# Grouped-query attention: two-pair-deep PV, K transposes after PV, and q transposed on the tensor engine instead of by DMA

## The chip, the cores and the metric

One NeuronCore of one Trainium2 chip runs the whole program. The metric is device microseconds of one execution, lower is better.

In names of engines PE is TensorE, PEld the loading of its weights, DVE is VectorE, ACT is ScalarE, POOL is GpSimd and SP is the queue that issues the DMAs. S, PT, PV and the other short names are the steps of the kernel, explained below.

## The reference

```python
B, Hq, Hkv, Sq, Sk, D = 16, 32, 8, 16, 2048, 128     # q, k, v = normal * 0.05, bf16
k = jnp.repeat(k, Hq // Hkv, axis=1)
v = jnp.repeat(v, Hq // Hkv, axis=1)
scores = jnp.einsum("bhqd,bhkd->bhqk", q, k) * D ** -0.5
p = softmax(scores, axis=-1)
return jnp.einsum("bhqk,bhkd->bhqd", p, v)
```

Four query heads share one K/V head, so each K/V head serves 4 x 16 = 64 rows of q. There are 128 K/V heads. The kernel takes two at a time: 64 pairs, and each pair fills 128 rows. K and V are 134.2 MB, q and the output 2.1 MB each, so at least 138.4 MB must move.

## The kernel before

For every pair p, these steps run. `KT`: PE transposes the two K heads (32 matmuls with an identity) into staging banks of PSUM, and DVE evicts them (four `kte`). `S`: 8 matmuls give the scores. `max`: DVE scales the scores into SBUF and finds the minimum of the negated scores. `exp`: ACT. `PT`: PE transposes P (16 matmuls), ACT evicts them (two `pte`). `PV`: 32 matmuls. `norm`: O is multiplied by the reciprocal of the row sum. The order is fixed on each engine:

```python
    for kk in range(0, last_std + 1):          # PE
        if kk < NP:
            pe_prog.append(("S", kk))
        if kk >= 1:
            pe_prog.append(("PT", kk - 1))
        pe_kt(kk)                               # both K transposes of pair kk + 2
        if kk >= 1:
            pe_prog.append(("PV", kk - 1))
    ...
    for kk in range(0, last_std + 1):          # ACT
        if kk >= 1:
            act_prog += pte(kk - 1)
        if kk < NP:
            act_prog.append(("exp", kk))
        if kk >= 1:
            act_prog.append(("norm", kk - 1))
```

All transposes share three staging banks (`NSTAGE = 3`), so a transpose of 8 tiles waits until the bank filled three steps earlier has been evicted:

```python
            def wait_bank_free(ld):
                u = ld["u"]
                if u >= NSTAGE:
                    prev = loads[u - NSTAGE]
                    pe.wait_ge(sem_ev[prev["eng"]], prev["eidx"])
```

q arrives already transposed, 512 rows (four pairs) at a time, by a DMA transpose. K has 8 buffers (4 pairs), V 12 (6 pairs); at step t the SP queue issues K(t), then V(t - DV), then the store of t - DSTORE:

```python
            def issue_q(c):
                sp.dma_start_transpose(QT[:, qch * c:qch * (c + 1)], qf[qch * c:qch * (c + 1), :]).then_inc(sem_q[c], 16)
```

## Time and profile before

| | before |
|---|---|
| time, median of 13 runs | 380.33 us (379.37 to 380.83) |
| PE / DVE / ACT busy | 86% / 81% / 72% |
| start of the first S, of the last S | 8.65 us, 367.6 us |
| gap from one S to the next, steady | 5.60 us |
| last V packet landed | 365.3 us of a 379.0 us span |

Busy times of the page of the kernel before, then its DMA rows (busy tenths and GB/s in 40 equal slices of the span), then its chain of waits by engine (shares of the span).

```profile
PE 325.3 (86%) x5632; PEld 257.3 (68%) x5632; DVE 307.9 (81%) x453; ACT 272.5 (72%) x316; POOL 1.0 (0%) x6
...
DMA  7999999999999999999999999999999999999950
GB/s 253 343 405 345 407 409 350 410 340 408 363 397 406 345 408 347 404 412 346 412 342 407 366 389 405 354 406 346 412 406 345 411 339 414 406 409 410 408 201 12
...
PE 56%; ACT 30%; DMA 6%; issue 3%; SPq 2%; DVE 1%
```

The DMA digits are 9 throughout, yet the bytes moved swing between about 410 and 345 GB/s. Where the rate is low, a q transpose is in flight: from the fourth slice to the last dip, each low slice comes about 12 us after SP issued a transpose, which is the median time from its issue to its landing, and the slices in which SP issues one run at 404 to 412. So the stream slows with the transfer, not with the issuing. The digits alone would hide that. The Trainium skill ("Perfetto Trace Analysis", "Identifying the Most-Contended Engine") warns that occupancy is misleading for DMA because there are 16 DMA engines; this trace agrees that it misleads, with the same digit 9 at 410 and at 345 GB/s.

The chain of waits of the kernel before between 150 and 185 us: start, length, and what that piece was. One loop of it is shown.

```profile
161.86 1.95 ACT PT L394 x2
163.81 0.14 issue
163.94 1.05 PE ST_ps L300 x16
165.00 1.01 PE O_ps L343 x32
166.01 0.86 PE S_ps L312 x8
166.87 0.57 PE ST_ps L328 x8
167.44 0.02 issue
```

These seven pieces add up to 5.60 us. PE waits for ACT to evict the P transposes, because K transposes need the same three banks (L300 are K transposes, L328 P transposes, L343 PV, L312 S). Then the waits view of the kernel before (who waited for whom: us in total, times, longest):

```profile
ACT PT L394 <- PE ST_ps L328: 66.1, 61, 3.1
DVE Sneg L374 <- PE S_ps L312: 55.7, 62, 2.0
PE ST_ps L300 <- ACT PT L394: 34.3, 113, 0.4
```

No engine is full; each waits for another once per loop.

### The profile page before, as it was taken

What the parts mean: (1) busy time and instruction counts of PE and PEld (TensorE: products, weight loads), DVE (VectorE), ACT (ScalarE), POOL (GpSimd) and SP (SyncE); (2) the same over time, 40 slices, a digit from 0 to 9 for tenths busy, and PEclk for the clock granted to TensorE, in tenths of its full rate; (3) what the DMA queues carried; (4) which work ended last, traced back from release to release, by engine and by line L of the source; (5) the groups of instructions that cost most, each with busy time, mean ns of one, the idle gap of its engine ahead of it and who ended that gap; (6) DMA issues with size and microseconds to landing.
All of it is one profiled execution on the core that took longest, in us unless ns stands there. A gap on an engine that the chain in (4) does not pass through costs nothing.

```text
span 379.0 us, 12914 instructions
## 1 busy us (share of the span) xinstructions
PE 325.3 (86%) x5632; PEld 257.3 (68%) x5632; DVE 307.9 (81%) x453; ACT 272.5 (72%) x316; POOL 1.0 (0%) x6
## 2 busy tenths in 40 slices
PE   4779889889889988888889889889888988988884
PEld 3567667677676776676767677677776766776664
DVE  2958888888898898787988888898898897898675
ACT  1357877877787787676877877787787786787882
POOL 1000000000000000000000000000000000000000
PEclk9989999999999999999999999999999999999999
DMA  7999999999999999999999999999999999999950
GB/s 253 343 405 345 407 409 350 410 340 408 363 397 406 345 408 347 404 412 346 412 342 407 366 389 405 354 406 346 412 406 345 411 339 414 406 409 410 408 201 12
DMA packets 54839, 139.25 MB, mean 367 GB/s; under 512 B 22016, under 2 KB 22016, under 8 KB 54784
## 3 DMA queue, kind: packets, MB, share of 16 engines
q1 hardware_dynamic: 54784, 138.43, 100.4%
q8 instruction: 45, 0.74, 0.8%
q14 instruction: 10, 0.08, 0.1%
HBM read 134.22 MB, written 2.10 MB: 360 GB/s over the span
## 4 chain that ended last, share of the span: by engine, by line
PE 56%; ACT 30%; DMA 6%; issue 3%; SPq 2%; DVE 1%
ACT PT L394 30%; PE O_ps L343 17%; PE ST_ps L300 16%; PE S_ps L312 14%; PE ST_ps L328 9%; DMA Kn<-in_k_dram 6%; SPq L234 1%; SPq L243 1%; DVE PT L364 1%; ACT KT L394 1%; DVE Sneg L374 0%; SPq L251 0%; DVE O L385 0%
## 5 line engine op out<-in xcount | busy, mean ns | idle before, releaser
L374 DVE TENSOR_SCALAR_CACHE_REDUCE Sneg<-S_ps 128x2048 f32<-128x2048 f32 x64 | 146.6, 2291 | 55.7 <-PE S_ps L312 55.7
L300 PE MATMUL ST_ps<-ident,Kn 128*128 128x128 bf16 x2048 | 147.7, 222 | 44.0 <-ACT PT L394 34.3
L394 ACT ACTIVATE PT<-ST_ps 128x1024 bf16<-128x1024 bf16 x124 | 120.2, 1021 | 66.1 <-PE ST_ps L328 66.1
L364 DVE COPY KT<-ST_ps 128x1024 bf16<-128x1024 bf16 x254 | 157.9, 681 | 7.7 <-PE ST_ps L300 7.7
L300 PEld LDWEIGHTS ST_ps<-ident,Kn 128*128 128x128 bf16 x2048 | 119.8, 98 | 65.2 <-issue 32.7
L398 ACT ACTIVATE P<-Sneg,nbias 128x2048 bf16<-128x2048 f32 x64 | 128.2, 2003 | 11.0 <-DVE Sneg L374 11.0
L328 PEld LDWEIGHTS ST_ps<-ident,P 128*128 128x128 bf16 x1024 | 57.3, 98 | 26.5 <-issue 25.2
L343 PE MATMUL O_ps<-Vb,PT 128*64 128x128 bf16 x2048 | 70.7, 222 | 5.2 <-ACT PT L394 1.9
L328 PE MATMUL ST_ps<-ident,P 128*128 128x128 bf16 x1024 | 68.5, 220 | 0.5 <-ACT KT L394 0.4
L343 PEld LDWEIGHTS O_ps<-Vb,PT 128*64 128x64 bf16 x2048 | 60.0, 111 | 12.5 <-DVE PT L364 2.6
L312 PE MATMUL S_ps<-KT,QT 128*64 128x512 bf16 x512 | 66.2, 379 | 1.8 <-DVE KT L364 0.9
L409 ACT ACTIVATE O<-O_ps,rrec 128x128 bf16<-128x128 f32 x61 | 22.4, 367 | 21.6 <-PE O_ps L343 21.6
L312 PEld LDWEIGHTS S_ps<-KT,QT 128*64 128x64 bf16 x512 | 25.9, 110 | 15.1 <-issue 2.3
L398 ACT ACTIVATION_READ_ACCUMULATOR P<-Sneg,nbias 128x1 f32 x64 | 12.8, 200 | 0.0
L368 DVE RECIPROCAL rrec<-rowsum 128x1 f32<-128x1 f32 x64 | 9.7, 152 | 3.2 <-ACT P L398 3.2
L374 DVE DVE_READ_ACCUMULATOR Sneg<-S_ps 128x1 f32 x64 | 5.3, 83 | 0.0
L385 DVE TENSOR_SCALAR O<-O_ps,rrec 128x128 bf16<-128x128 f32 x3 | 1.0, 348 | 2.5 <-PE O_ps L343 2.5
L394 ACT ACTIVATE KT<-ST_ps 128x1024 bf16<-128x1024 bf16 x2 | 1.9, 1020 | 1.3 <-PE ST_ps L300 1.3
L364 DVE COPY PT<-ST_ps 128x1024 bf16<-128x1024 bf16 x4 | 2.6, 684 | 0.1
L398 ACT ACT_TABLE_LOAD x1 | 1.3, 1283 | 0.7 <-PEq L424 0.7
L229 POOL TENSOR_SCALAR ident<-iota_t 128x128 bf16<-128x128 int32 x1 | 0.5, 535 | 0.1
L227 POOL IOTA iota_t<- 128x128 int32 x1 | 0.2, 234 | 0.4 <-POOLq L424 0.4
(4 smaller groups left out, 0.4 us busy)
## 6 DMA issues: line engine op xcount, KB each, us to landing
Kn<-in_k_dram SPq DMA_DIRECT2D x128, 512.0 KB, 13.0
Vb<-in_v_dram SPq DMA_DIRECT2D x128, 512.0 KB, 12.8
out_dram<-O SPq DMA_DIRECT2D x64, 32.0 KB, 12.5
QT<-in_q_dram SPq DMA_TRANSPOSE x16, 12.2
```

The costliest lines, as they stand in the source:

```text
L234: sp.dma_start_transpose(QT[:, qch * c:qch * (c + 1)], qf[qch * c:qch * (c + 1), :]).then_inc(sem_q[c], 16)
L243: sp.dma_start(Kn[s][:, :, :], k[b, h].rearrange("(a j) d -> a j d", j=J)).then_inc(sem_k[s], 16)
L300: ins = pe.transpose(stage_ap(ld["bank"], t), Kn[s][:, j, :], ident[:, :])
L312: ins = pe.matmul(S_ps[64 * gg:64 * (gg + 1), 512 * c:512 * (c + 1)], QT[:, 128 * p + 64 * gg:128 * p + 64 * (gg + 1)], kt[:, gg, 4 * c:4 ...
L328: ins = pe.transpose(stage_ap(ld["bank"], t), P[p % 2][:, 128 * j:128 * (j + 1)], ident[:, :])
L343: ins = pe.matmul(O_ps[64 * gg:64 * (gg + 1), 0:128], pt[:, j, 64 * gg:64 * (gg + 1)], Vb[g % NBV][:, j, :], start=(j == 0), stop=(j == J ...
L364: dve.tensor_copy(evac_dst(ld), stage_bank_ap(ld["bank"])).then_inc(sem_ev["dve"], 1)
L368: dve.reciprocal(rrec[:, p:p + 1], rowsum[:, p:p + 1]).then_inc(sem_rec, 1)
L374: dve.tensor_scalar(Sneg[kk % 2][:, :], S_ps[:, :], -scale, None, op0=ALU.mult, op1=ALU.min, accum_out=nbias[:, kk:kk + 1],).then_inc(sem_ ...
L394: act.activation(evac_dst(ld), stage_bank_ap(ld["bank"]), ACT.Copy).then_inc(sem_ev["act"], 1)
L398: act.activation(P[kk % 2][:, :], Sneg[kk % 2][:, :], ACT.Exp, bias=nbias[:, kk:kk + 1], scale=-1.0, accum_out=rowsum[:, kk:kk + 1],).then ...
L409: act.activation(Osb[s_][:, :], O_ps[:, 0:128], ACT.Copy, scale=rrec[:, p:p + 1]).then_inc(sem_nm["act"], 1)
```

## The change

It has two parts. The new loop comes from `hand_schedule`: PV moves one more pair behind (a third PT buffer), norm goes from ACT to DVE, and in odd cycles one of the four K evictions goes to ACT. Secondly q is loaded by a plain DMA and transposed on PE. V is issued 3 pairs behind K, not 2. A list scheduler (`build_schedule`) is also added, but never called. The core of the diff, cuts marked:

```diff
+NPT = 3
-DV = 2
+DV = 3
...
+def hand_schedule(NP, qp, pe_transposes_q):
+    """One pattern for every pair k: S(k) PT(k-1) KT(k+1,1) PV(k-2) KT(k+2,0)."""
...
+    for k in range(NP + 2):
+        if k < NP:
+            pe.append(("S", k))
+            dve.append(("max", k))
...
+        if 1 <= k <= NP:
+            pe.append(("PT", k - 1))
+            act.append(("pte", k - 1, 0))
+            (act if k < NP else dve).append(("pte", k - 1, 1))
+        if k >= 2:
+            pe.append(("PV", k - 2))
+        if k >= 1:
+            kt(k + 1, 1), kte(dve, k + 1, 1)
+        if k >= 2:
+            dve.append(("norm", k - 2))
+        kt(k + 2, 0)
+        kte(dve, k + 2, 0, (0,))
+        if k % 2 == 0:
+            kte(dve, k + 2, 0, (1,))
+        if k < NP:
+            dve.append(("recip", k))
+            act.append(("exp", k))
+        if k % 2 == 1:
+            kte(act, k + 2, 0, (1,))
+        if k % qp == qp - 3:
+            qt(k // qp + 1)
...
-                sp.dma_start_transpose(QT[:, qch * c:qch * (c + 1)], qf[qch * c:qch * (c + 1), :]).then_inc(sem_q[c], 16)
+                sp.dma_start(Qn[:, 4 * c:4 * (c + 1), :], qf[qch * c:qch * (c + 1), :].rearrange("(a j) d -> a j d", j=4)).then_inc(sem_q[c], 16)
...
+                elif op[0] == "QT":
...
+                    for j in range(4):
+                        ins = pe.transpose(stage_ap(ld["bank"], j), Qn[:, 4 * c + j, :], ident[:, :])
```

More of the change, by code (lines that the diff above doesn't have):

```diff
@@ L20 @@
 QLEAD = 6
+_DUR = {
+    "KT_load": 0.46, "PT_load": 0.46, "S": 0.75, "PV": 1.02,
+    ("dve", "kte"): 0.63, ("dve", "pte"): 0.63, ("dve", "max"): 2.30, ("dve", "recip"): 0.17, ("dve", "norm"): 0.36,
+    ("act", "kte"): 1.07, ("act", "pte"): 1.07, ("act", "exp"): 2.08, ("act", "norm"): 0.46,
+    "K": 0.65, "V": 0.65, "ST": 0.65, "Q": 3.3,
+}
+_LAT = 0.12
+_LAT_SAME = 0.04
+_DMA_LAT = 2.0
+_BW = 0.371
+_BW_SLOW = 0.364
+_RING_MB = 5.2
+_SIZE = {"K": 0.5, "V": 0.5, "Q": 0.25 * 1.45, "ST": 0.03125 * 1.45}
@@ new lines, with sp_program @@
+_T0 = 7.0
+def sp_program(NP, qch_pairs, dv=DV, dstore=DSTORE, qlead=QLEAD):
+    sp = []
+    n_qch = (NP + qch_pairs - 1) // qch_pairs
+    q_step = {c: max(0, c * qch_pairs - qlead) for c in range(n_qch)}
+    for t in range(NP + max(dv, dstore) + 1):
+        if t < NP:
+            sp += [("K", 2 * t), ("K", 2 * t + 1)]
+        for c in range(n_qch):
+            if q_step[c] == t:
+                sp.append(("Q", c))
+        if 0 <= t - dv < NP:
+            sp += [("V", 2 * (t - dv)), ("V", 2 * (t - dv) + 1)]
+        if 0 <= t - dstore < NP:
+            sp.append(("ST", t - dstore))
+    return sp
@@ new lines, with build_schedule, t, eng_options @@
+SCHED_OPTS = dict(kte_engs=("dve", "act"), pte_engs=("dve", "act"), norm_engs=("dve", "act"), eft=True)
+def build_schedule(NP, qch_pairs, nbk=NBK, nbv=NBV, nbo=NBO, nkt=NKT, npt=NPT, nstage=NSTAGE, opts=None):
+    INF = float("inf")
+    DUR = _DUR
+    opts = dict(SCHED_OPTS, **(opts or {}))
+    sp = sp_program(NP, qch_pairs)
+    done = {}
+    def t(key):
+        return done.get(key, INF)
+    pe_left = []
+    for p in range(NP):
+        pe_left += [("KT", p, 0), ("KT", p, 1), ("S", p), ("PT", p), ("PV", p)]
+    x_left = []
+    for p in range(NP):
+        x_left += [("kte", p, gg, h) for gg in range(2) for h in range(2)]
+        x_left += [("pte", p, h) for h in range(2)]
+        x_left += [("max", p), ("recip", p), ("exp", p), ("norm", p)]
+    sp_left = list(sp)
+    progs = {"pe": [], "dve": [], "act": [], "sp": []}
+    free = {"pe": _T0, "dve": _T0, "act": _T0, "sp": _T0}
+    load_u = {}
+    next_u = [0]
+    dma_fast_end = [0.0]
+    dma_slow_end = [0.0]
+    dma_hist = []
+    issued_mb = [0.0]
+    pe_sched = set()
+    timeline = []
+    def eng_options(op):
+        k = op[0]
+        if k in ("max", "recip"):
+            return ("dve",)
+        if k == "exp":
+            return ("act",)
+        if k == "kte":
+            return opts["kte_engs"]
+        if k == "pte":
+            return opts["pte_engs"]
+        return opts["norm_engs"]
+    def ready_pe(op):
+        kind = op[0]
+        r = []
+        if kind == "KT":
+            p, gg = op[1], op[2]
+            r.append(t(("dma", "K", 2 * p + gg)))
+            if p >= nkt and ("S", p - nkt) not in pe_sched:
+                return INF
+            u0 = next_u[0]
+            for h in range(2):
+                if u0 + h >= nstage:
+                    r.append(t(("evac", u0 + h - nstage)))
+        elif kind == "S":
+            p = op[1]
+            r.append(t(("dma", "Q", p // qch_pairs)))
+            for gg in range(2):
+                for hh in range(2):
+                    key = ("KT", p, gg, hh)
+                    if key not in load_u:
+                        return INF
+                    r.append(t(("evac", load_u[key])))
+            if p >= 1:
+                r.append(t(("max", p - 1)))
+        elif kind == "PT":
+            p = op[1]
+            r.append(t(("exp", p)))
+            if p >= npt and ("PV", p - npt) not in pe_sched:
+                return INF
+            u0 = next_u[0]
+            for h in range(2):
+                if u0 + h >= nstage:
+                    r.append(t(("evac", u0 + h - nstage)))
+        elif kind == "PV":
+            p = op[1]
+            for hh in range(2):
+                key = ("PT", p, None, hh)
+                if key not in load_u:
+                    return INF
+                r.append(t(("evac", load_u[key])))
+            for gg in range(2):
+                r.append(t(("dma", "V", 2 * p + gg)))
+            if p >= 1:
+                r.append(t(("norm", p - 1)))
+        return max(r) if r else 0.0
+    def ready_x(op):
+        kind = op[0]
+        r = []
+        if kind == "kte":
+            key = ("KT", op[1], op[2], op[3])
+            if key not in load_u:
+                return INF
+            r.append(t(("load", load_u[key])))
+        elif kind == "pte":
+            key = ("PT", op[1], None, op[2])
+            if key not in load_u:
+                return INF
+            r.append(t(("load", load_u[key])))
+        elif kind == "max":
+            p = op[1]
+            r.append(t(("S", p)))
+            if p >= 2:
+                r.append(t(("exp", p - 2)))
+        elif kind == "recip":
+            r.append(t(("exp", op[1])))
+        elif kind == "exp":
+            p = op[1]
+            r.append(t(("max", p)))
+            if p >= 2:
+                r.append(t(("PT", p - 2)))
+        elif kind == "norm":
+            p = op[1]
+            r += [t(("PV", p)), t(("recip", p))]
+            if p >= nbo:
+                r.append(t(("dma", "ST", p - nbo)))
+        return max(r) if r else 0.0
+    def ring_ok_time(size):
+        need = issued_mb[0] + size - _RING_MB
+        if need <= 0:
+            return 0.0
+        for tm, cum in dma_hist:
+            if cum >= need:
+                return tm
+        return dma_hist[-1][0] if dma_hist else 0.0
+    def ready_sp(op):
+        kind, x = op
+        r = [ring_ok_time(_SIZE[kind])]
+        if kind == "K":
+            if x >= nbk:
+                r.append(t(("KT", (x - nbk) // 2, (x - nbk) % 2)))
+        elif kind == "V":
+            if x >= nbv:
+                r.append(t(("PV", (x - nbv) // 2)))
+        elif kind == "ST":
+            r.append(t(("norm", x)))
+        return max(r) if r else 0.0
+    KIND_PRIO = {"S": 0, "max": 0, "exp": 0, "PT": 1, "pte": 1, "PV": 2, "recip": 2, "norm": 2, "KT": 3, "kte": 3}
+    while pe_left or x_left or sp_left:
+        best = None
+        if sp_left:
+            op = sp_left[0]
+            rd = ready_sp(op)
+            if rd < INF:
+                st = max(free["sp"] + _LAT_SAME, rd + _LAT)
+                best = ((round(st, 3), -1, -1), st, "sp", op)
+        seen = 0
+        for op in pe_left:
+            rd = ready_pe(op)
+            if rd == INF:
+                continue
+            st = max(free["pe"] + _LAT_SAME, rd + _LAT)
+            cand = ((round(st, 3), op[1], KIND_PRIO[op[0]]), st, "pe", op)
+            if best is None or cand[0] < best[0]:
+                best = cand
+            seen += 1
+            if seen > 12:
+                break
+        seen = 0
+        for op in x_left:
+            rd = ready_x(op)
+            if rd == INF:
+                continue
+            engs = eng_options(op)
+            if opts["eft"] and len(engs) > 1:
+                fin = [(max(free[e] + _LAT_SAME, rd + _LAT) + DUR[(e, op[0])], e) for e in engs]
+                fin.sort()
+                engs = (fin[0][1],)
+            for eng in engs:
+                st = max(free[eng] + _LAT_SAME, rd + _LAT)
+                cand = ((round(st, 3), op[1], KIND_PRIO[op[0]]), st, eng, op)
+                if best is None or cand[0] < best[0]:
+                    best = cand
+            seen += 1
+            if seen > 24:
+                break
+        assert best is not None, "scheduler stuck"
+        _, st, eng, op = best
+        kind = op[0]
+        if eng == "sp":
+            sp_left.pop(0)
+            en = st + DUR[kind]
+            size = _SIZE[kind]
+            sf = max(en + (_DMA_LAT if dma_fast_end[0] < en else 0.0), dma_fast_end[0])
+            dma_fast_end[0] = sf + size / _BW
+            ssl = max(en + (_DMA_LAT if dma_slow_end[0] < en else 0.0), dma_slow_end[0])
+            dma_slow_end[0] = ssl + size / _BW_SLOW
+            comp = max(dma_fast_end[0], dma_slow_end[0])
+            done[("dma", kind, op[1])] = comp
+            issued_mb[0] += size
+            dma_hist.append((comp, issued_mb[0]))
+        elif eng == "pe":
+            pe_left.remove(op)
+            pe_sched.add(op)
+            if kind in ("KT", "PT"):
+                en = st
+                for h in range(2):
+                    uu = next_u[0]
+                    next_u[0] += 1
+                    key = ("KT", op[1], op[2], h) if kind == "KT" else ("PT", op[1], None, h)
+                    load_u[key] = uu
+                    if h == 1 and uu >= nstage:
+                        en = max(en, t(("evac", uu - nstage)) + _LAT)
+                    en = en + DUR[kind + "_load"]
+                    done[("load", uu)] = en
+                done[(kind, op[1], op[2]) if kind == "KT" else (kind, op[1])] = en
+            else:
+                en = st + DUR[kind]
+                done[(kind, op[1])] = en
+        else:
+            x_left.remove(op)
+            en = st + DUR[(eng, kind)]
+            if kind == "kte":
+                done[("evac", load_u[("KT", op[1], op[2], op[3])])] = en
+            elif kind == "pte":
+                done[("evac", load_u[("PT", op[1], None, op[2])])] = en
+            else:
+                done[(kind, op[1])] = en
+        free[eng] = en
+        progs[eng].append(op)
+        timeline.append((st, en, eng, op))
+    info = dict(timeline=timeline, done=done, end=max(max(free.values()), dma_slow_end[0]))
+    return dict(pe=progs["pe"], dve=progs["dve"], act=progs["act"], sp=progs["sp"], info=info)
@@ new lines, in hand_schedule, with kt, kte, qt @@
+def hand_schedule(NP, qp, pe_transposes_q):
+    n_qch = (NP + qp - 1) // qp
+    pe, dve, act = [], [], []
+    def kt(p, gg):
+        if p < NP:
+            pe.append(("KT", p, gg))
+    def kte(prog, p, gg, halves=(0, 1)):
+        if p < NP:
+            prog.extend(("kte", p, gg, h) for h in halves)
+    def qt(c):
+        if pe_transposes_q and c < n_qch:
+            pe.append(("QT", c))
+            act.append(("qte", c))
+    kt(0, 0), kt(0, 1), kte(dve, 0, 0), kte(dve, 0, 1), qt(0)
+    for k in range(NP + 2):
+        if k < NP:
+            pe.append(("S", k))
+            dve.append(("max", k))
+        if k == 0:
+            kt(1, 0), kt(1, 1), kte(dve, 1, 0), kte(dve, 1, 1)
+        if 1 <= k <= NP:
[19 more added lines that the diff above has]
+            qt(k // qp + 1)
+    return dict(pe=pe, dve=dve, act=act, sp=sp_program(NP, qp))
@@ L53, in bass_standalone__gqa_softmax__sampling_kernel @@
     QT = sb("QT", [128, NROWS], BF16)
+    Qn = sb("Qn", [128, NROWS // 128, 128], BF16)
     Kn = [sb(f"Kn{i}", [128, J, 128], BF16) for i in range(NBK)]
@@ L58, in bass_standalone__gqa_softmax__sampling_kernel @@
     P = [sb(f"P{i}", [128, Sk], BF16) for i in range(2)]
-    PT = [sb(f"PT{i}", [128, J, 128], BF16) for i in range(2)]
+    PT = [sb(f"PT{i}", [128, J, 128], BF16) for i in range(NPT)]
     Osb = [sb(f"O{i}", [128, 128], BF16) for i in range(NBO)]
@@ L81, in bass_standalone__gqa_softmax__sampling_kernel @@
     sem_nm = {"dve": sem("sem_normd"), "act": sem("sem_norma")}
-    tail = NP >= 6
-    a_, b_, c_ = NP - 3, NP - 2, NP - 1
-    def kt_cycle(p):
-        if p == 0:
-            return -1
-        if p == 1:
-            return 0
-        if tail and p >= b_:
-            return p - 1
-        return p - 2
-    kt_in_cycle = {c: [] for c in range(-1, NP + 1)}
-    for p in range(NP):
-        kt_in_cycle[kt_cycle(p)].append(p)
-    pe_prog, dve_prog, act_prog = [], [], []
-    def pe_kt(c):
-        for p in kt_in_cycle[c]:
-            pe_prog.extend([("KT", p, 0), ("KT", p, 1)])
-    def kte(p, gg=None):
-        ggs = [gg] if gg is not None else [0, 1]
-        return [("kte", p, g2, h) for g2 in ggs for h in range(2)]
-    def pte(p):
-        return [("pte", p, h) for h in range(2)]
-    last_std = (a_ if tail else NP)
-    pe_kt(-1)
-    for kk in range(0, last_std + 1):
-        if kk < NP:
-            pe_prog.append(("S", kk))
-        if kk >= 1:
-            pe_prog.append(("PT", kk - 1))
-        pe_kt(kk)
-        if kk >= 1:
-            pe_prog.append(("PV", kk - 1))
-    if tail:
-        pe_prog += [("S", b_), ("KT", c_, 0), ("KT", c_, 1), ("PT", a_)]
-        pe_prog += [("S", c_), ("PT", b_), ("PV", a_), ("PV", b_)]
-        pe_prog += [("PT", c_), ("PV", c_)]
-    dve_prog += kte(0)
-    for kk in range(0, last_std + 1):
-        if kk >= 1:
-            dve_prog.append(("recip", kk - 1))
-        if kk < NP:
-            dve_prog.append(("max", kk))
-        for p in kt_in_cycle[kk]:
-            dve_prog += kte(p)
-    if tail:
-        dve_prog += [("recip", a_), ("max", b_)] + kte(c_, 1)
-        dve_prog += [("recip", b_), ("max", c_)] + pte(b_) + [("norm", a_)]
-        dve_prog += [("norm", b_), ("recip", c_)] + pte(c_) + [("norm", c_)]
-    for kk in range(0, last_std + 1):
-        if kk >= 1:
-            act_prog += pte(kk - 1)
-        if kk < NP:
-            act_prog.append(("exp", kk))
-        if kk >= 1:
-            act_prog.append(("norm", kk - 1))
-    if tail:
-        act_prog += kte(c_, 0) + [("exp", b_)] + pte(a_)
-        act_prog += [("exp", c_)]
+    sched = hand_schedule(NP, pairs_per_qch, True)
+    pe_prog, dve_prog, act_prog, sp_prog = sched["pe"], sched["dve"], sched["act"], sched["sp"]
     loads = []
@@ L151, in bass_standalone__gqa_softmax__sampling_kernel @@
     pt_loads = {}
+    q_loads = {}
     for op in pe_prog:
@@ L166, in bass_standalone__gqa_softmax__sampling_kernel @@
                 pt_loads[(p, h)] = ld
+        elif op[0] == "QT":
+            ld = dict(kind="QT", pair=op[1], gg=None, half=0, u=len(loads), eng=None, eidx=None)
+            ld["bank"] = ld["u"] % NSTAGE
+            loads.append(ld)
+            q_loads[op[1]] = ld
     def op_load(op):
@@ L172, in op_load @@
             return pt_loads[(op[1], op[2])]
+        if op[0] == "qte":
+            return q_loads[op[1]]
         return None
@@ L259, in issue_store @@
                 ocnt[s] += 1
-            q_issue_step = {c: max(0, c * pairs_per_qch - QLEAD) for c in range(n_qch)}
-            for t in range(NP + max(DV, DSTORE) + 1):
-                if t < NP:
-                    for gg in range(2):
-                        issue_k(grp(t, gg))
-                for c in range(n_qch):
-                    if q_issue_step[c] == t:
-                        issue_q(c)
-                if 0 <= t - DV < NP:
-                    for gg in range(2):
-                        issue_v(grp(t - DV, gg))
-                if 0 <= t - DSTORE < NP:
-                    issue_store(t - DSTORE)
+            for op in sp_prog:
+                kind, x = op
+                if kind == "K":
+                    issue_k(x)
+                elif kind == "V":
+                    issue_v(x)
+                elif kind == "Q":
+                    issue_q(x)
+                else:
+                    issue_store(x)
             for s in range(NBO):
@@ L301, in _ @@
                         ins.then_inc(sem_stage, 1)
+                elif op[0] == "QT":
+                    c = op[1]
+                    pe.wait_ge(sem_q[c], 16)
+                    ld = q_loads[c]
+                    wait_bank_free(ld)
+                    for j in range(4):
+                        ins = pe.transpose(stage_ap(ld["bank"], j), Qn[:, 4 * c + j, :], ident[:, :])
+                    ins.then_inc(sem_stage, 1)
                 elif op[0] == "S":
                     _, p = op
-                    pe.wait_ge(sem_q[(128 * p) // qch], 16)
-                    for sm, n in evac_waits([kt_loads[(p, gg, h)] for gg in range(2) for h in range(2)]):
+                    for sm, n in evac_waits([kt_loads[(p, gg, h)] for gg in range(2) for h in range(2)] + [q_loads[(128 * p) // qch]]):
                         pe.wait_ge(sm, n)
@@ L338, in _ @@
                         pe.wait_ge(*norm_wait(p - 1))
-                    pt = PT[p % 2]
+                    pt = PT[p % NPT]
                     for j in range(J):
@@ L355, in evac_dst @@
                 return KT[p % NKT][:, ld["gg"], 8 * h:8 * (h + 1), :]
-            return PT[p % 2][:, 8 * h:8 * (h + 1), :]
+            return PT[p % NPT][:, 8 * h:8 * (h + 1), :]
         @block.vector
@@ L393, in _ @@
                     act.wait_ge(sem_stage, ld["u"] + 1)
+                    if ld["kind"] == "QT":
+                        c, b0 = ld["pair"], ld["bank"] * 1024
+                        act.activation(
+                            QT[:, qch * c:qch * (c + 1)].rearrange("p (i j) -> p i j", j=4),
+                            ST_ps[:, b0:b0 + 512].rearrange("p (j i) -> p i j", j=4), ACT.Copy,
+                        ).then_inc(sem_ev["act"], 1)
+                        continue
                     act.activation(evac_dst(ld), stage_bank_ap(ld["bank"]), ACT.Copy).then_inc(sem_ev["act"], 1)
@@ L397, in _ @@
                     act.wait_ge(sem_max, kk + 1)
+                    if kk >= 2:
+                        act.wait_ge(sem_stage, pt_loads[(kk - 2, 1)]["u"] + 1)
                     act.activation(
```

## The prediction

> **What bounds the kernel now.** One in-order loop of the compute engines, not one full engine. Between starts of successive score matmuls S(k) the timeline shows 5.60 us for nearly all 63 gaps, so 8.65 us (first S) + 359 us + 11.4 us (tail) = the 379 us span. The chain of waits is 56% PE and 30% ACT; the loop in it is: P transposes 0.57, ACT evicts them 1.95, then 0.14, K transposes 1.05, PV 1.01, S 0.86, and 0.02 = 5.60 us. DVE is 81% busy, PE 86%, ACT 72%; DVE waits 55.7 us for S, ACT 66.1 us for P transposes (waits view). The DMA is second: its slices alternate between about 408 and 345 GB/s, the low ones at the 16 DMA transposes of q. A transpose thus costs an estimated 1.4 us of transfer time over its bytes (about 60 GB/s lost in a 9.5 us slice). DMA waits of PE are small; the largest makes one early gap 8.92 us.
>
> **What changes.** (1) PV moves a pair later (PV(k-2), three PT buffers), and K transposes are split around it, so evictions run under other PE work: the serial ACT wait leaves the loop. (2) All norms move from ACT to DVE (0.35 us); in odd cycles one K eviction moves to ACT (0.97 instead of 0.62). (3) q comes by plain DMA and is transposed on PE (4 matmuls) and evicted by ACT, every fourth cycle.
>
> **Sums per pair**, back-to-back rates from the timeline. PE: 0.90 + 1.96 + 0.91 + 0.96 = 4.73 us. DVE: 2.37 (max) + 3.5 x 0.62 + 0.34 + 0.16 = 5.04. ACT: 1.94 + 2.2 + 0.49 + about 0.15 (q) = 4.8. DMA: 2.16 MB at 410 GB/s = 5.28. Following one cycle with these durations and the 0.1-0.15 us hand-over seen now, even and odd cycles take about 5.23 and 5.03 us; the q transpose holds a stage bank and delays ACT, an estimated 0.8 us every fourth cycle. So about 5.33 us per pair, just above the DMA's 5.28. The gain is only 0.27 us of 5.60, although the serial ACT wait was 1.95.
>
> Ends: S(1) starts near 15 us (15.6 now), the second gap falls from 8.92 to one period; the tail is about 12 us. Span = 15.2 + 62 x 5.33 + 12 = 357.7 us; the time lies 1.5 us above the span: 359 us.
>
> The Trainium skill ("DMA: Bandwidth & Descriptors", "Latency and other measured facts") gives DMA transposes 261 GB/s, about 350-400 when contiguous. This trace suggests far less, an estimated 131 KB in 1.7 us = 76 GB/s.
>
> **Prediction:** 359 us, 350 to 369 in 8 of 10 cases. Faster by over 2%: 0.94; within 2%: 0.05; slower: 0.01.
>
> **What shows it right.** S-to-S gaps near 5.0-5.3 us with a longer one every fourth; GB/s flat near 400-410 with no dips; ACT's wait for P transposes down from 66 to under 25 us, DVE's for S from 56 to under 20 us; DVE over 88% and PE about 90% busy; chain with DVE or DMA in place of ACT evictions.
>
> **What would make it wrong.** The DMA sustains less than 400 GB/s: then waits for Kn or Vb appear in the steady state and the time goes to 365-370. Three stage banks couple the engines more tightly: gaps of 5.5. Or the q stage hides fully and the loop reaches 5.1: about 348, unless DMA holds it at 5.28.

## The result

The changed kernel takes 358.17 us (median of 8 runs, 357.69 to 358.91) against 380.33. The ratio is 0.9422, 95% interval 0.9412 to 0.9431. Ratios here are the mean time of one kernel's fast runs over the mean of the other's fast runs in the same rounds, so they are not quite the ratio of the medians.

Busy times, DMA rows and the chain of waits (shares of the span) from the page of the changed kernel:

```profile
PE 332.9 (93%) x5696; PEld 262.7 (74%) x5696; DVE 308.1 (86%) x482; ACT 289.8 (81%) x303; POOL 1.0 (0%) x6
...
DMA  7999999999999999999999999999999999999950
GB/s 298 412 408 404 410 408 412 410 406 412 409 411 411 407 412 409 411 409 408 410 412 409 408 409 410 411 412 407 411 392 411 409 403 398 411 412 412 394 219 13
...
PE 65%; DMA 24%; DVE 3%; SPq 2%; ACT 2%; issue 2%
```

The dips are gone: the stream runs at about 410 GB/s almost from start to end. ACT, which held 30% of the chain before, now holds 2%, and the DMA went from 6% to 24%. The waits view of the changed kernel (L594 are P transposes, L578 S, L609 PV, L559 K transposes):

```profile
ACT PT L667 <- PE ST_ps L594: 46.6, 48, 2.0
...
DVE Sneg L640 <- PE S_ps L578: 14.0, 27, 1.6
...
PE O_ps L609 <- DMA Vb<-in_v_dram: 3.6, 9, 0.6
...
PE ST_ps L559 <- ACT PT L667: 0.6, 2, 0.4
```

PE's 34.3 us of waiting for ACT's evictions of P are gone from the head of this list (0.6 us are left). In its place PV waits for V. The timeline of the changed kernel shows two of these waits (start, length, what; in brackets the idle time before it and what ended it):

```profile
158.01 1.08 PE L609 MATMUL O_ps<-Vb,PT 128*64 128x128 bf16 x32 [0.21 <-DMA Vb<-in_v_dram]
...
163.49 1.08 PE L609 MATMUL O_ps<-Vb,PT 128*64 128x128 bf16 x32 [0.41 <-DMA Vb<-in_v_dram]
```

Starts of S in this trace: the first at 9.12 us, the last at 343.29 us, so 334.2 / 63 = 5.30 us per pair. Early gaps are 5.00 us with 5.41 each fourth; after some 65 us many are 5.3 to 6.2. The last V packet lands at 347.2 us of the 356.2 us span. The time is where the prediction put it. The question is whether it is there for the predicted reason: is it the compute loop (predicted 5.33 us per pair) or the DMA stream (2.16 MB per pair at 410 GB/s = 5.28 us) that sets it? The total cannot tell them apart.

### The profile page after: what moved, and what is told of

Read it like the earlier page. It is cut to its first block, busy times and chain, and to the rows that moved or that the text cites. A ratio compares the mean times of both kernels' runs of the same rounds, so it can differ in the third digit from the quotient of the medians.

```text
span 356.2 us, 13135 instructions
## 1 busy us (share of the span) xinstructions
PE 332.9 (93%) x5696; PEld 262.7 (74%) x5696; DVE 308.1 (86%) x482; ACT 289.8 (81%) x303; POOL 1.0 (0%) x6
## 4 chain that ended last, share of the span: by engine, by line
PE 65%; DMA 24%; DVE 3%; SPq 2%; ACT 2%; issue 2%
PE ST_ps L559 24%; DMA Vb<-in_v_dram 23%; PE O_ps L609 14%; PE S_ps L578 13%; PE ST_ps L594 12%; DVE KT L630 2%; ACT PT L667 2%; PE ST_ps L567 2%; DVE Sneg L640 1%; SPq L513 1%; SPq L496 1%; DMA Kn<-in_k_dram 1%; ACT P L673 1%; DVE O L651 0%; SPq L505 0%
## 5 line engine op out<-in xcount | busy, mean ns | idle before, releaser
L630 DVE COPY KT<-ST_ps 128x1024 bf16<-128x1024 bf16 x225 | 145.5, 683 | 24.7 <-PE ST_ps L559 24.6
L667 ACT ACTIVATE PT<-ST_ps 128x1024 bf16<-128x1024 bf16 x127 | 123.2, 1022 | 46.9 <-PE ST_ps L594 46.6
L559 PE MATMUL ST_ps<-ident,Kn 128*128 128x128 bf16 x2048 | 132.2, 222 | 7.0 <-DMA Kn<-in_k_dram 4.3
L559 PEld LDWEIGHTS ST_ps<-ident,Kn 128*128 128x128 bf16 x2048 | 116.3, 98 | 17.9 <-issue 6.3
L594 PEld LDWEIGHTS ST_ps<-ident,P 128*128 128x128 bf16 x1024 | 57.3, 98 | 29.3 <-ACT P L673 15.1
L609 PE MATMUL O_ps<-Vb,PT 128*64 128x128 bf16 x2048 | 72.2, 223 | 6.7 <-DMA Vb<-in_v_dram 3.6
L609 PEld LDWEIGHTS O_ps<-Vb,PT 128*64 128x64 bf16 x2048 | 61.4, 111 | 15.3 <-issue 9.4
L594 PE MATMUL ST_ps<-ident,P 128*128 128x128 bf16 x1024 | 68.5, 220 | 3.2 <-ACT P L673 2.5
L578 PE MATMUL S_ps<-KT,QT 128*64 128x512 bf16 x512 | 67.7, 385 | 3.1 <-DVE KT L630 1.6
L578 PEld LDWEIGHTS S_ps<-KT,QT 128*64 128x64 bf16 x512 | 23.6, 109 | 25.4 <-DVE KT L630 4.2
L667 ACT ACTIVATE KT<-ST_ps 128x1024 bf16<-128x1024 bf16 x31 | 31.2, 1006 | 0.1
L651 DVE TENSOR_SCALAR O<-O_ps,rrec 128x128 bf16<-128x128 f32 x64 | 21.8, 341 | 2.9 <-PE O_ps L609 2.9
L662 ACT ACTIVATE QT<-ST_ps 128x512 bf16<-128x512 bf16 x16 | 9.4, 589 | 6.4 <-PE ST_ps L567 6.4
L567 PE MATMUL ST_ps<-ident,Qn 128*128 128x128 bf16 x64 | 6.4, 223 | 1.0 <-issue 0.2
L567 PEld LDWEIGHTS ST_ps<-ident,Qn 128*128 128x128 bf16 x64 | 4.1, 99 | 3.1 <-issue 3.0
```

The source lines that it names most:

```text
L559: ins = pe.transpose(stage_ap(ld["bank"], t), Kn[s][:, j, :], ident[:, :])
L567: ins = pe.transpose(stage_ap(ld["bank"], j), Qn[:, 4 * c + j, :], ident[:, :])
L578: ins = pe.matmul(S_ps[64 * gg:64 * (gg + 1), 512 * c:512 * (c + 1)], QT[:, 128 * p + 64 * gg:128 * p + 64 * (gg + 1)], kt[:, gg, 4 * c:4 ...
L594: ins = pe.transpose(stage_ap(ld["bank"], t), P[p % 2][:, 128 * j:128 * (j + 1)], ident[:, :])
L609: ins = pe.matmul(O_ps[64 * gg:64 * (gg + 1), 0:128], pt[:, j, 64 * gg:64 * (gg + 1)], Vb[g % NBV][:, j, :], start=(j == 0), stop=(j == J ...
L630: dve.tensor_copy(evac_dst(ld), stage_bank_ap(ld["bank"])).then_inc(sem_ev["dve"], 1)
```

## The experiments

Theory A: the stream binds the changed kernel, and its compute loop alone would be faster. Theory B' is the prediction's sum: the compute loop binds at 5.33 us and the stream is just below. For the kernel before, theory A has loop and stream about level; its rival B says that q's DMA transposes were the main cost. The experiments were measured in three batches, each beside the kernel before, which took 380.09, 380.11 and 380.01 us in them.

### 1. Only the q path on the old loop (q_only)

```diff
 pe_kt(-1)
+pe_prog.append(("QT", 0)); act_prog.append(("qte", 0))
 ...                                    # per cycle kk, PE after PV, ACT after norm
+if kk % 4 == 1 and kk // 4 + 1 < n_qch:
+    ...                                # QT(kk // 4 + 1) on PE, its eviction on ACT
...
-sp.dma_start_transpose(QT[...], qf[...])
+sp.dma_start(Qn[...], qf[...])
```

> The kernel before with only the q path of the change: plain DMA, 4 PE transposes and one ACT eviction per four pairs; order of the loop, norms and PT buffers as before. Theory A (after the change the DMA stream binds, before it the in-order loop of 5.60 us and the DMA stream were about equal): the loop stays at 5.60 us, the few DMA stalls (about 6 us in all) go, the q stage adds about 0.3 us every fourth cycle: 379 us, within 1.5% of before, GB/s flat near 386 with SP waiting for K buffers. Theory B (q transposes were the main cost, loop order did not matter): about 358-362 us.

Measured: 382.97 us, ratio 1.0064 (1.0044 to 1.0084). It is even a little slower, and 4 us above theory A's 379. The GB/s row of this run:

```profile
GB/s 301 411 408 406 408 407 411 408 408 410 411 410 410 409 408 411 406 398 378 405 391 398 366 386 370 384 382 376 399 363 374 396 376 377 364 384 377 97 6 12
```

The stream runs at 410 until the buffers are full, then falls to the 380 or so that a loop of 5.60 us consumes, and ends at 357 us of a 381 us span. So the bandwidth set free could not be used. The gaps read 6.03, 5.63, 5.60, 5.60: the q stage adds 0.43 us in each fourth cycle (15 x 0.43 = 6.5 us), more than the vanished DMA stalls gave back. Theory B falls.

### 2. Only the new loop, q still by DMA transposes (loop_only)

```diff
-hand_schedule(NP, pairs_per_qch, True)
+hand_schedule(NP, pairs_per_qch, False)
...
-sp.dma_start(Qn[...], qf[...])
+sp.dma_start_transpose(QT[...], qf[...])
```

> The changed kernel with only the q path undone: q comes by DMA transposes again and PE and ACT do no q work. Theory A: the DMA needs (8.65 MB at 410 GB/s + 1.4 us) / 4 = 5.63 us per pair, so S-to-S gaps average 5.6, PE waits for Kn or Vb, time 376-380 us: nearly the whole gain is lost. Theory B' (the compute loop binds in the changed kernel, DMA only just below): without q work on PE and ACT the loop falls to 5.1 us, time 345-352 us.

Measured: 374.0 us, ratio 0.9834 (0.9819 to 0.9849). GB/s row and waits of PE for DMA in this run:

```profile
GB/s 257 348 407 342 403 362 397 406 342 405 347 413 406 339 412 347 410 406 346 412 341 412 394 363 409 350 406 352 403 404 345 410 344 410 407 408 413 404 411 61
...
PE O_ps L610 <- DMA Vb<-in_v_dram: 9.4, 11, 2.0
PE ST_ps L559 <- DMA Kn<-in_k_dram: 6.4, 4, 4.7
```

The new loop, with less work on PE and ACT than the changed kernel, is 16 us slower than it. B' expected 345 to 352 us and falls; theory A's 376 to 380 was 2 us too high. The last V lands at 364.9 us, 0.4 us from where the kernel before had it: the stream with transposes in it was already about as long as the old loop needed. The 6.1 us that this run gains lie after that landing: from there to the end of the span the kernel before takes 13.7 us, this run 7.6. Between this run and the changed kernel the last landing moves by 17.7 us, 1.1 us for each of 16 transposes above what a plain load costs.

The two parts together (times in us):

| | q by DMA transpose | q by plain DMA and PE |
|---|---|---|
| old loop | 380.1 | 383.0 |
| new loop | 374.0 | 358.2 |

Alone they are worth -6.1 and +2.9; together -22. Two limits stood at the same height, and each part lowers only one.

### 3. Half the traffic, same work (no_v, before_no_v)

V is loaded into its 12 buffers once and never again. The result is wrong (relative error 1.17), the compute work is not touched.

```diff
                 if g >= NBV:
+                    return
...
-pe.wait_ge(sem_v[g % NBV], 16 * (g // NBV + 1))
+pe.wait_ge(sem_v[g % NBV], 16)
```

> The changed kernel with V loaded only into the first 12 buffers and never again (wrong result on purpose); all compute work unchanged. The DMA moves half as much. Theory A: the free compute loop shows, gaps 5.00, 5.00, 5.00, 5.41, mean 5.10, time about 9 + 63 x 5.10 + 13 + 1.5 = 345 us. Theory B' (the prediction's own sum, compute at 5.33 us per pair): 358 us, unchanged.

> The kernel before with V loaded only into the first 12 buffers (wrong result on purpose). Theory A: its loop keeps 5.60 us because three quarters of the loop are PE work and serial ACT evictions: about 374 us (8.65 + 63 x 5.60 + 10.4 + 1.5), 1 to 2% below before. If the DMA stream had been its main limit: about 345-350 us as for the changed kernel.

Measured: no_v 346.11 us (ratio 0.9093, 0.9062 to 0.9123); before_no_v 376.62 us (0.9907, 0.9890 to 0.9924). Theory A had 345 and 374 us, B' 358 for no_v. The new loop has 12 us that only the V traffic takes from it; the old has 3.5 us. In before_no_v the gaps stay at 5.60. In no_v they are 5.00, 5.00, 5.00, 5.41, a mean of 5.10. PE's timeline of no_v, in the cycle with the q stage (L610 PV, L560 K transposes, L568 q transposes, L579 S, L595 P transposes):

```profile
157.75 1.05 PE L579 MATMUL S_ps<-KT,QT 128*64 128x512 bf16 x8
158.74 1.07 PE L595 MATMUL ST_ps<-ident,P 128*128 128x128 bf16 x16
159.74 1.08 PE L610 MATMUL O_ps<-Vb,PT 128*64 128x128 bf16 x32
160.75 2.02 PE L560 MATMUL ST_ps<-ident,Kn 128*128 128x128 bf16 x32
162.84 0.38 PE L568 MATMUL ST_ps<-ident,Qn 128*128 128x128 bf16 x4
163.16 1.05 PE L579 MATMUL S_ps<-KT,QT 128*64 128x512 bf16 x8
```

The view lists no wait in it. One short pause is there all the same: the q transposes start 0.28 us after the last K transpose, where 0.06 us is usual. DVE's eviction of a bank ended 0.14 us before they start, so this is probably the wait for that bank; it makes up about 0.2 us of the 0.41 us of the q stage. The chain of waits of this run, by engine (shares of the span), says the same:

```profile
PE 94%; ACT 2%; DVE 1%; DMA 1%; issue 1%
```

So in the other cycles the free loop is bound by PE issuing without a pause: 0.99 (S) + 1.00 (PT) + 1.01 (PV) + 2.00 (KT) = 5.00 us. The prediction had 4.73 for this sum, and DVE as the longest.

Where the missing 0.27 us lie can be read from the starts of successive matmuls in no_v, between 60 and 300 us (medians, worked out from the trace's records):

```
transpose -> transpose   56 ns      S -> P transpose    312 ns (S itself streams 213)
P transpose -> PV       149 ns      PV -> K transpose   152 ns (PV -> S was 53 before)
K transpose -> S        194 ns
```

Transposes use all 128 columns of the array, PV and S two halves of 64 (128\*128 and 128\*64 in the trace). Each change between the two costs 93 to 138 ns. The old order (S, PT, KT, PV) changes twice in a loop, the new one (S, PT, PV, KT) four times. Two more at 0.1 and 0.14 give 0.24 us of the 0.27. The Trainium skill ("TensorEngine Tiling (Array Packing)", "Key Properties") says that a change of tiling mode drains the TensorE; this trace fits that, with the figure above, but does not show that the pause is a drain and not, say, the load of weights of the other shape. No run with PV moved next to S was made, so what it would save is an estimate.

### 4. Without the q stage, full traffic (no_qt)

Only the first chunk of q is transposed and evicted, and S reads it for every pair; all chunks are still loaded.

```diff
-        if pe_transposes_q and c < n_qch:
+        if pe_transposes_q and c < 1:
...                                     # S waits for the first chunk alone
-QT[:, 128 * p + 64 * gg:128 * p + 64 * (gg + 1)],
+QT[:, 128 * (p % 4) + 64 * gg:128 * (p % 4) + 64 * (gg + 1)],
```

> The changed kernel with the PE transposes and ACT evictions of q done only for the first chunk (S reads that chunk for all pairs, wrong result on purpose); every q chunk is still loaded. Theory A (DMA stream binds): 358 us, within 0.5% of the changed kernel. Theory B' (the q stage costs 0.8 us every fourth cycle on the critical path, as the prediction had it): 358 - 15 x 0.8 = 346 us.

Measured: 358.0 us, ratio 0.9417 (0.9403 to 0.9431), the same as the changed kernel. PE and ACT work was removed and nothing was gained, which is what a stream-bound kernel does. (The comparison with the reference passes although the q is wrong: with inputs scaled by 0.05 the scores are so small that softmax is nearly uniform. In this case a pass says little about the q path.)

### 5. More traffic, same work (q_twice, q_twice_b)

Each q chunk is loaded a second time into a place that nobody reads. The first attempt reused one scratch tile and waited for it:

```diff
 sp.dma_start(Qn[...], qf[...]).then_inc(sem_q[c], 16)
+if c:
+    sp.wait_ge(sem_x, 16 * c)
+sp.dma_start(Qx[:, :, :], qf[...]).then_inc(sem_x, 16)
```

> The changed kernel with every q chunk loaded a second time by a plain DMA into a scratch tile that nobody reads: 2.1 MB more on the same queue. Theory A: 2.1 MB / 0.41 = 5.1 us longer, 363 us. Theory B': the compute loop hides it, within 1 us of 358.

Measured: 366.18 us, 8.0 above the changed kernel's 358.17, more than expected. The timeline showed a flaw of the experiment: at the start two chunks are issued in a row, so the SP queue stood still from about 3 to 6.3 us waiting for the scratch load, and the first slice moved 202 GB/s, not 298. The mended version gives every chunk its own place, without waits, and doubles chunks 2 to 15:

```diff
                     issue_q(x)
+                    if x >= 2:
+                        sp.dma_start(Qx[:, 4 * x:4 * (x + 1), :], ...).then_inc(sem_x, 16)
```

> q_twice without its flaw: there the SP queue waited at the start (3.3 us at 2.6 to 6.3 us) for a scratch load, so 2 of the 8 us were not traffic. Here chunks 2 to 15 are loaded twice, each into a scratch place of its own, with no wait: 14 loads x 131 KB = 1.84 MB. Theory A: by bytes at 410 GB/s +4.5 us, by the time of the 1 KB packets in the trace (6.0 us for 16 loads) +5.2 us, so about 363 us. If other waits of the queue caused the 8 us: 365-366 us.

Measured: 362.07 us beside 358.04 us for the changed kernel in the same rounds: 4.0 us for 1.84 MB, or 0.29 us for a chunk of 131 KB, near the 4.5 us that the bytes give at 410 GB/s. In the traces the last K or V packet lands at 352.1 us, against 346.8 in the changed kernel of the same rounds: the stream itself is 5.3 us longer, as the packet times gave (5.2), and what follows the landing is 1.6 us shorter in this run (not explained). Traffic that no engine reads lengthens the stream by its full transfer time. B' (no cost) falls once more.

### 6. Using it: a shorter tail (lag3, lag4, lag4_tail)

If the stream is the floor, what is left is the time after it: 347.2 to 356.2 us in the changed kernel. Putting V further behind K makes the last K land earlier, so that the last S, max and exp are done when the last V arrives. PV then runs L pairs behind S:

```diff
-    for k in range(NP + 2):
+    for k in range(NP + L):
-        if k >= 2: pe.append(("PV", k - 2))
+        if k >= L: pe.append(("PV", k - L))        # and norm likewise
-DV = 3          # L + 1
-DSTORE = 7      # L + 5
-NPT = 3         # 3 for L = 3, 4 for L = 4
-if k % qp == qp - 3:
+if k % qp == qp - 3 and k < NP:
```

> The changed kernel with PV one more pair behind (PV(k-3)), V loads one more pair behind K (4 instead of 3), stores one step later. Theory A: the stream's end does not move (last V lands at about 347 us), but the last K lands one V pair (2.6 us) earlier and so does the last S: 355-356 us, 2 to 3 us below the changed kernel. Otherwise unchanged or slower by one more PV at the end.

> The same with PV two more pairs behind (PV(k-4), V loads 5 pairs behind K, four PT buffers). Theory A: the last K lands 5.2 us earlier than in the changed kernel, 353-355 us; the floor is the last V's landing plus PV, norm and store, about 351 + 1.5 us. If the V buffers (12) or PT buffers bind instead: no faster than lag3.

Measured: lag3 356.85 us (ratio 0.9382, 0.9365 to 0.9400), lag4 355.29 us (0.9342, 0.9326 to 0.9357). Both gain, each a little less than expected. The last V lands at 346.9 and 347.0 us: the stream has not moved. The end of lag4's timeline shows what ate the rest:

```profile
343.35 1.89 PE L594 MATMUL ST_ps<-ident,P 128*128 128x128 bf16 x16 [2.55 <-ACT P L673]
...
345.16 1.78 PE L609 MATMUL O_ps<-Vb,PT 128*64 128x128 bf16 x32
...
347.48 1.08 PE L609 MATMUL O_ps<-Vb,PT 128*64 128x128 bf16 x32 [0.54 <-DVE O L651]
...
349.10 1.08 PE L609 MATMUL O_ps<-Vb,PT 128*64 128x128 bf16 x32 [0.54 <-DVE O L651]
...
350.72 1.08 PE L609 MATMUL O_ps<-Vb,PT 128*64 128x128 bf16 x32 [0.54 <-DVE O L651]
```

Four PVs queue up behind the last P transposes, each waiting for the norm before it, while PE had idled 2.55 us for the last exp. So lag4_tail does PV(60) and PV(61) in that idle time:

```diff
+        if k == NP - 1:
+            pe.extend(("PV", p) for p in (NP - 4, NP - 3))      # norms likewise on DVE, before the last recip
+        if k in (NP, NP + 1):
+            pe.append(("PV", k - 2))
```

> lag4 with the last PVs reordered: PV(60) and PV(61) and their norms go before the transposes of the last P (PE waited 2.55 us for the last exp there) instead of after them, so only PV(62) and PV(63) follow. Theory A: the end is then set by the last V's landing (347.0 us) + PV 1.1 + norm 0.35 + store about 2.7: span near 351.5, time 352-353.5 us. If the end is still set by the serial tail and not by the stream: no better than lag4's 355.3.

> The same kernel as the run called lag4, on the same chip and rounds as lag4_tail, for the comparison: 355.3 us within 1 us.

> The changed kernel itself, on the same chip and rounds as lag4_tail, for the comparison: 358.2 us within 1 us.

Measured in the same rounds: lag4_tail 353.14 us (ratio 0.9294, 0.9281 to 0.9307), lag4 again 356.28 us (0.9369, 0.9354 to 0.9384), the changed kernel again 358.04 us (0.9417, 0.9401 to 0.9432). The last PV of lag4_tail, in its timeline:

```profile
347.61 1.08 PE L617 MATMUL O_ps<-Vb,PT 128*64 128x128 bf16 x32 [1.36 <-DMA Vb<-in_v_dram]
```

Now the last V itself is awaited. Its last packet lands at 346.9 us and the span ends at 351.0 us, 4.1 us later. This version beats both kernels; what remains is the stream plus one PV, norm and store.

## Why the prediction was right or wrong

The time was right: 359 us predicted, 358.17 measured, range 350 to 369. The reason given for it was only half right.

- Right: the kernel before was an in-order loop of 5.60 us. It keeps 5.60 us when half the traffic is taken away (376.62 us).
- Right: the serial wait for ACT's evictions left the loop, dips in GB/s vanished, the DMA came into the chain of waits, PE was 93% busy, and DVE's wait for S fell to 14 us (predicted under 20). Wrong among the signs: ACT's wait for P transposes fell only to 46.6 us (predicted under 25), and DVE was 86% busy (predicted over 88%). That fits a loop in which neither is the limit; even in no_v, where PE is, ACT still waits 35.9 us.
- Wrong: "K transposes are split around it". I read this in the docstring; in the code, PV comes first and both K transposes after it.
- Wrong: "PE: ... = 4.73 us". The durations were taken from an order with two changes of matrix shape in a loop; the new order has four. No_v shows 5.00 us, and PE, not DVE, as the longest engine.
- Wrong: the q stage, "an estimated 0.8 us every fourth cycle". It is 0.41 us in no_v (gaps of 5.41 and 5.00), and costs nothing at all in the changed kernel (no_qt: 358.0 us).
- Wrong, and it decides: "about 5.33 us per pair, just above the DMA's 5.28". The compute loop is 5.10 us per pair, below the stream. (The prediction's even and odd cycles, 5.23 and 5.03, are 5.00 in no_v; its 0.8 every fourth cycle is 0.41.) The stream binds, and the measured mean of 5.30 is its 5.28, not the loop's 5.33. The two numbers were so close that the wrong one gave the right time; that was luck. The prediction named this case among its doubts ("unless DMA holds it at 5.28").
- Size: 1.4 us per transpose over its bytes was somewhat high. Between loop_only and the changed kernel the last landing moves 1.1 us per transpose over a plain load; the time moves 15.8 / 16 = 1.0 us.
- Not settled: part of the 12 us between no_v and the changed kernel are not waits for V. Between 20 and 340 us PV starts later after the P transposes than the usual 149 ns by about 6.6 us in all; the waits view puts 3.6 us of this down to V. Seven more steps, of 0.27 to 1.03 us, lie inside a run of matmuls of one kind, where the program has no wait; they cost some 3.6 us over the usual steps (the profile lists five of them, 2.4 us, as idle with no cause). No_v has none of these in that stretch; loop_only has nine that the profile lists, 7.2 us in sum. All seven begin 1.5 to 2.2 us after the start of a 16 KB packet of the instruction queue, of which there are 46, and end 2.4 to 2.6 us after it, so late instruction fetches behind a saturated stream are a candidate; no run tested this.

## What to carry to other kernels

When two limits stand at about the same height, neither change alone pays much and both together do, so cost each part against the other limit before you drop it as useless. A right total proves no mechanism: take away half the traffic, then take away some of the work, and see which of them moves the time. When a stream has become the floor, look at what is left after its last byte, and order the last loads and steps so that only the shortest chain follows it.

## What the Trainium skill lacked or had wrong

- "DMA: Bandwidth & Descriptors", "Latency and other measured facts": it gives DMA transposes 261 GB/s, and about 350 to 400 when contiguous. Here, in a full queue, a transpose of 131 KB cost 1.1 us more than a plain load by the last landings (1.0 by the times), and that load 0.38 us (0.29): 1.5 us (1.3), an estimated 88 to 102 GB/s for the transpose.
- "TensorEngine Tiling (Array Packing)", "Key Properties": it says that a change of mode drains the array, without a figure. Here a change between full 128-column transposes and 64-column matmuls cost 93 to 138 ns in successive matmul starts.
- No page says that PE can pause inside a run of matmuls while the DMA is saturated: seven pauses, some 3.6 us, in the changed kernel between 20 and 340 us, none in no_v. If late instruction fetches are the cause, which is open, it belongs to "Runtime: NRT & Kernel Launch", "Instruction fetch mechanics".
